# One attention group's values projected ahead of the others, VectorE's exponentials from the first unit on, and the last output tiles spread over three engines

## The chip, the cores and the metric

The kernel runs on one core of a Trainium2 chip. The metric is the device time of one execution in microseconds (us); where a kernel ran several times the median is given.

## The reference

One input x (2048 x 512, bf16) goes through two branches, which a gate mixes for each row:

```python
g = sigmoid((x * gate_w).sum(-1, keepdims=True))
qkv = x @ wqkv                     # 32 heads of 16
p = softmax(q @ k.T * 16 ** -0.5)  # for each head, 2048 x 2048
a = concat_heads(p @ v) @ wo
b = (silu(x @ w_gate) * (x @ w_up)) @ w_down   # 512 -> 1792 -> 512
return g * a + (1 - g) * b
```

The costly part is the exponential of 32 x 2048 x 2048 scores.

## The kernel before

The program is laid out by a planner in Python that runs while the program is built. It keeps estimated clocks of TensorE, ScalarE and VectorE and decides what each engine does next. The scores are cut into 32 *units* (a block of 512 queries with a group of four heads). A unit has 16 *slots* (one tile of 128 keys, four heads: four score tiles of 128 x 512). Group 0 comes first for all four query blocks, so units 0 to 3 are slots 0 to 63. Most score tiles go in pairs to ScalarE (`e_t`). Some go in blocks of four to VectorE, which computes the exponential from integer and half-precision operations (`y_t`). Everything else (projections, gated network, output matmuls) is cut into pieces, and a pacer fits them between score matmuls so that each is done by its deadline.

```python
def v_pieces(tt, act_evac=False):      # values of ALL groups for key tile tt
    ... 4 matmuls of 128x512: lhsT=xT[:, dc, tile tt], rhs=wv[:, dc, :]
    # copied to vaug by ScalarE (act_evac) or by VectorE, later
...
# the start: the key group and its bound (the stabiliser of the softmax)
act(out=q0r, in_=qp0, func=ACT.Copy)
for i in range(2):
    vec.tensor_reduce(out=kpart0[:, i:i + 1], in_=kp0[i], op=ALU.max, apply_absolute_value=True)
    v_now(i)                           # value tile i, copied by ScalarE
    act(out=kaug[...half i...], in_=kp0[i], func=ACT.Identity, bias=ones_h[i], scale=1.0)
    ...
v_now(2); (bound matmul bp0); (two additions on VectorE); v_now(3)
...
for tt in range(4, 16):                # the other value tiles, needed at slot tt
    v_chain[tt] = pace.add(v_pieces(tt), 0, tt + 3)
f0, f1 = 44, SLOTS - 8                 # the network is paced from slot 44
...
def to_vector():                       # may VectorE take the next score tile?
    un, at_ = divmod(nxt, 4 * KT)      # unit, position 0..63 in it
    ...
    if not un or at_ > (50 if un < UNITS - 1 else 4) or y_live[0] >= 3 or sum(v[0] for v in vops) > 6:
        return 0
    return 1
...
last_mm(1, on_l)                       # four last matmuls, tq = 0, 1, 2, 3
for tq in range(TQ):
    store(qb * TQ + tq, a_ps[tq], acc[0][:, tq, :], mt[:, tq, :])   # VectorE addition, store by SyncE
```

Of the kernel before, what the change touches and what calls it, by code (L numbers as in the profile page):

```python
# [78 lines left out]
def kernel(  # L79
# [100 lines left out]

    rb = big.tile([P, NB, QBW], BF16, name="rb")
    wv = rb[:, :, :]

    nc.sync.dma_start(out=wv, in_=A_wqkv[:, 2 * D:3 * D].rearrange("(dc p) c -> p dc c", p=P))
    for c0 in (D, 0):
        nc.sync.dma_start(out=wqk[:, :, c0 + 64:c0 + D],
                          in_=A_wqkv[:, c0 + 64:c0 + D].rearrange("(dc p) c -> p dc c", p=P))
# [39 lines left out]
    for g in range(1, G):  # L227

        nc.vector.memset(kaug[:, g, :].bitcast(F32), 1.0019378662109375)
    vaug = big.tile([P, KT, G * 4 * VC + 16], BF16, name="vaug")  # L230
    nc.gpsimd.memset(vaug[:, :, G * 4 * VC:], 0.0)
    nc.gpsimd.memset(
        vaug[:, :, 0:G * 4 * VC].rearrange("p t (h c) -> p t h c", c=VC)[:, :, :, 0:1], 1.0)

# [5 lines left out]
    for h in range(8):  # L240
        c = 2 * (h % 4) + h // 4
        nc.gpsimd.memset(lo_t[:, c:c + 1], float(DH * h))
    far_t = const.tile([P, 8], F32, name="far_t")

    nc.vector.tensor_scalar(out=lo_t[:], in0=lo_t[:], scalar1=pidx[:, 0:1], scalar2=None, op0=ALU.subtract)
    nc.vector.tensor_scalar(out=far_t[:], in0=lo_t[:], scalar1=-float(DH) + 0.5, scalar2=-1.0,
                            op0=ALU.is_gt, op1=ALU.mult)
    nc.vector.scalar_tensor_tensor(out=bsel[:, :], in0=lo_t[:], scalar=0.5, in1=far_t[:],
                                   op0=ALU.is_lt, op1=ALU.mult)
    nc.gpsimd.memset(wo_l[:], 0.0)  # L250
    sbc_t = const.tile([P, P], BF16, name="sbc_t")
    nc.gpsimd.memset(sbc_t[:], 0.0)
# [125 lines left out]
        vec.tensor_scalar(out=kneg[:, b, :], in0=bsel[:, :], scalar1=kb[:, b:b + 1],  # L378
                          scalar2=None, op0=ALU.mult)

    def v_pieces(tt, act_evac=False):
        st = {}

        def pc(h):
            def f():
                if h == 0:
                    st["p"] = m_tile("vp")
                for dc in (2 * h, 2 * h + 1):
                    mm(st["p"][:, 0:D], lhsT=xT[:, dc, tt * P:(tt + 1) * P], rhs=wv[:, dc, :],
                       start=(dc == 0), stop=(dc == DC - 1))  # L390
                spend("F", 2)
                if h == 1 and act_evac:
                    end()
                elif h == 1:
                    later(0.75, end)
            return f

        def end():
            dst = vaug[:, tt, 0:G * 4 * VC].rearrange("p (h c) -> p h c", c=VC)[:, :, 1:1 + DH]
            sv = st["p"][:, 0:D].rearrange("p (h c) -> p h c", c=DH)  # L400
            if act_evac:
                act(out=dst, in_=sv, func=ACT.Copy)
            else:
                vec.tensor_copy(out=dst, in_=sv)
            m_free(plan.pe if act_evac else plan.dve)
        return [(2, pc(0), True), (2, pc(1), False)]


# [311 lines left out]
    def pv(bs, last):  # L720


        un = bs[0] // (4 * KT)
        extra = un < closed
        if extra:
            o = m_tile("x_ps")
        else:
            if un not in o_of:
                while un and un - 1 not in osbs:
                    pay()  # L730
                plan.pe = max(plan.pe, o_end[0])
                o_of[un] = ps_o.tile([P, QBW], F32, tag="o", name="o_ps")
            o = o_of[un]
        for b in bs:
            n, j = b // 4, HEADS[b % 4]
            first = extra or (un, j) not in begun
            begun.add((un, j))
            c0 = (4 * UNIT[un][1] + j) * VC
            if n < KT and n in v_chain:
                force(v_chain[n])  # L740
            mm(o[32 * j:32 * j + 32, :], lhsT=vaug[:, n % KT, c0:c0 + 32], rhs=e_of.pop(b),
               start=first, stop=extra or last, tile_position=(0, 32 * j), skip_group_check=True)
            e_left.pop(b, None)
        spend("C", 1, max(e_end.pop(b, 0.0) for b in bs))
        if extra:
            def add():
                blocks[un] -= 1
                vec.tensor_tensor(out=(of_of if blocks[un] else osbs)[un][:, :], in0=of_of[un][:, :], in1=o[:, :],
                                  op=ALU.add)
                m_free(plan.dve)  # L750
                if not blocks[un]:
                    finish(un)
            later(0.6, add)
# [116 lines left out]
    q0r = work.tile([P, QBW], BF16, tag="qst", name="q0r")  # L870
    kneg0 = mt[:, 3, P:2 * P]
    kneg1 = mt[:, 3, 2 * P:3 * P]
    def v_now(tt):
        for _, f, _ in v_pieces(tt, act_evac=True):
            f()

    act(out=q0r[:, :], in_=qp0[:, :], func=ACT.Copy)
    for i in range(2):
        vec.tensor_reduce(out=kpart0[:, i:i + 1], in_=kp0[i][:, :], axis=AX.X, op=ALU.max,
                          apply_absolute_value=True)  # L880
        vec.tensor_copy(out=ones_h[i][:], in_=onescol[:])
        v_now(i)
        act(out=kaug[:, 0, i * 2 * QBW:(i + 1) * 2 * QBW], in_=kp0[i][:, :], func=ACT.Identity,
            bias=ones_h[i][:, 0:1], scale=1.0)
        if i == 0:
            vec.tensor_scalar(out=kneg1, in0=bsel0, scalar1=kpart0[:, 0:1], scalar2=None, op0=ALU.mult)
            vec.tensor_scalar(out=aq0[:, :].bitcast(U16), in0=q0r[:, :].bitcast(U16), scalar1=0x7FFF, scalar2=None,
                              op0=ALU.bitwise_and)
    vec.scalar_tensor_tensor(out=kneg0, in0=bsel0, scalar=kpart0[:, 1:2], in1=kneg1,
                             op0=ALU.mult, op1=ALU.min)  # L890
    v_now(2)
    bp0 = ps_d.tile([P, QBW], F32, tag="d", name="bp0")
    mm(bp0[:, :], lhsT=kneg0, rhs=aq0[:, :], start=True, stop=True)
    for v in range(2):
# [1 line left out]
    for v in range(2):  # L896
        vec.scalar_tensor_tensor(out=q0[0][:, v, :], in0=bp0[:, :], scalar=vsel[:, v:v + 1],
                                 in1=q0[0][:, v, :], op0=ALU.mult, op1=ALU.add)
    V0 = 4
    v_now(3)  # L900
    plan.dve = plan.act = plan.pe


    pace = Pacer()
    need = {}
    v_chain = {}
    for tt in range(V0, KT):
        v_chain[tt] = pace.add(v_pieces(tt), 0, tt + 3)
    prev = []
    for qb in range(1, QB):  # L910
        d = qb * KT
# [29 lines left out]
    order_ = [(qb, fc) for qb in range(QB) for fc in range(FC)]  # L941
    prev = []
    fin_prev = []
    f0, f1 = 44, SLOTS - 8
    per = (f1 - f0) / QB
    for qb in range(QB):
        a0 = f0 + per * qb
# [65 lines left out]
    def pv_ready(now):  # L1013

        if late and (now is None or late[0][0] <= now):
            un = late[0][1][0] // (4 * KT)
            if un == closed or un < closed and (now is None or m_ready() is not None and m_ready() <= now):
                return late[0][1]
        if done < SLOTS and done // KT == closed and not (now is not None and done in v_chain
                                                          and not v_chain[done].done()):  # L1020
            bs = [b for b in range(4 * done, 4 * done + 4) if b not in vset]
            if all(b in e_of for b in bs) and (now is None or max(e_end[b] for b in bs) <= now):
                if closed in o_of or now is None or (not closed or closed - 1 in osbs) and o_end[0] <= now:
                    return bs
        return None

    def pvs_ready(now):

        k = n = 0
        for ready, bs in late[:2]:  # L1030
            un = bs[0] // (4 * KT)
            if ready <= now and (un == closed or un < closed and k == 0 and m_ready() is not None and m_ready() <= now):
                k += 1
        for n in (done, done + 1):
            if n < SLOTS and n // KT == closed and not (n in v_chain and not v_chain[n].done()):
                bs = [b for b in range(4 * n, 4 * n + 4) if b not in vset]
                if all(b in e_of for b in bs) and max(e_end[b] for b in bs) <= now and (
                        closed in o_of or (not closed or closed - 1 in osbs) and o_end[0] <= now):
                    k += 1
        return min(k, 2)  # L1040
# [27 lines left out]

    def side(most):

        c = pace.next(plan.slot) if pace.credit > 0 else None
        if c is None:
            return None
        mms, _, takes = c.pieces[c.i]
# [11 lines left out]
    def to_vector():  # L1086

        un, at_ = divmod(nxt, 4 * KT)
        if vcur:
            if nxt % 4 in [b % 4 for b in vcur["b"]]:  # L1090
                return 0
            return 2 if at_ >= 4 * KT - 4 * (NV - vcur["i"]) else 1
        if not un or at_ > (50 if un < UNITS - 1 else 4) or y_live[0] >= 3 or sum(v[0] for v in vops) > 6:
            return 0
        return 1

    while nxt < nb:
# [4 lines left out]
        if pairs[0] - min(e_left.values(), default=pairs[0]) >= EB - 1:  # L1102

            for m in (done, done + 1):
                while m in v_chain and not v_chain[m].out():
                    emit_piece(v_chain[m])
            next_pv()
            continue
        room = s_end[pairs[0] % 2] - plan.pe
# [56 lines left out]
    a_ps += [ps_m.tile([P, QBW], F32, tag="m", name="a_l")[:, :] for _ in range(2)]  # L1166

    def last_mm(w, on):
        for tq in range(TQ):
            mm(a_ps[tq][:, 0:D], lhsT=on[:, tq * P:(tq + 1) * P], rhs=wo_l[:, w, :], start=(w == 0), stop=(w == 1))  # L1170
    last_mm(0, osbs[un - 1])
    dt = ps_d.tile([P, QBW], F32, tag="d", name="dt")
# [12 lines left out]
        cs = slice(tq * P, (tq + 1) * P)  # L1185
        vec.tensor_tensor(out=on_l[:, cs], in0=osb[:, cs], in1=rps[:, cs], op=ALU.mult)
    last_mm(1, on_l)
    for tq in range(TQ):
        store(qb * TQ + tq, a_ps[tq], acc[0][:, tq, :], mt[:, tq, :])


# [28 lines left out]
```

## Time and profile before

| | before |
|---|---|
| median of 3 runs | 876.64 us (876.36 to 877.8) |
| span of the profiled run | 872.4 us |
| exponentials on ScalarE / blocks on VectorE | 882 / 71 |
| first exponential begins | 19.27 us |
| last exponential ends | 863.62 us |
| tail from there to the end | 8.8 us |

Three numbers make up the span: the *start* (up to the first exponential), the *middle* (from there to the end of the last one) and the *tail*. I also use one figure for the middle that I worked out from the trace's records. In every profile of this study the median step from the start of one exponential to the start of ScalarE's next instruction is 904 ns. What all steps have beyond 904 ns, added up, I call the *excess*; it is 20.0 us before. The middle is then 904 ns for each exponential, some 26.8 us for the 57 other ScalarE instructions, and the excess.

### The profile page before, as it was taken

What the parts mean: (1) busy time and instruction counts of PE and PEld (TensorE: products, weight loads), DVE (VectorE), ACT (ScalarE), POOL (GpSimd) and SP (SyncE); (2) the same over time, 40 slices, a digit from 0 to 9 for tenths busy, and PEclk for the clock granted to TensorE, in tenths of its full rate; (3) what the DMA queues carried; (4) which work ended last, traced back from release to release, by engine and by line L of the source; (5) the groups of instructions that cost most, each with busy time, mean ns of one, the idle gap of its engine ahead of it and who ended that gap; (6) DMA issues with size and microseconds to landing.
All of it is one profiled execution on the core that took longest, in us unless ns stands there. A gap on an engine that the chain in (4) does not pass through costs nothing.

```text
span 872.4 us, 14196 instructions
## 1 busy us (share of the span) xinstructions
PE 784.8 (90%) x5078; PEld 207.6 (24%) x5168; DVE 786.9 (90%) x1103; ACT 845.4 (97%) x947; POOL 7.1 (1%) x29
## 2 busy tenths in 40 slices
PE   6999999999999899999989888899898989989985
PEld 2222222222222222222222222222222222222221
DVE  6379999999999999999999999999999998999984
ACT  3999999999999999999999999999999999999995
POOL 3000000000000000000000000000000000000000
PEclk9999999999999999999999999999999999999999
DMA  8401121031101112210011121110011121000000
GB/s 208 111 1 28 29 50 38 21 69 28 31 11 26 40 33 73 52 37 11 4 31 31 34 55 45 42 28 4 4 25 36 36 57 48 21 10 4 5 20 24
DMA packets 87535, 31.98 MB, mean 37 GB/s; under 512 B 75120, under 2 KB 87016, under 8 KB 87464
## 3 DMA queue, kind: packets, MB, share of 16 engines
q1 hardware_dynamic: 86408, 30.94, 14.5%
q8 instruction: 40, 0.66, 0.3%
q10 hardware_dynamic: 1056, 0.13, 0.1%
q14 instruction: 31, 0.25, 0.1%
HBM read 20.83 MB, written 2.34 MB: 27 GB/s over the span
## 4 chain that ended last, share of the span: by engine, by line
ACT 42%; PE 34%; DVE 11%; issue 11%; SPq 1%; DMA 0%; ACTq 0%; DVEq 0%
ACT e_t L161 38%; PE s_t L158 13%; PE o_ps L158 7%; DVE y_t L167 5%; PE d_t L158 4%; PE dps L158 3%; ACT th L161 3%; DVE u_t L167 2%; PE gp L158 2%; PE qp L158 1%; PE up L158 1%; SPq L174 1%; PE kp L158 1%; DVE mt L167 1%; PE a_ps L158 1%
## 5 line engine op out<-in xcount | busy, mean ns | idle before, releaser
L161 ACT ACTIVATE e_t<-s_t 128x1024 bf16<-128x1024 f32 x882 | 821.9, 1079 | 4.8 <-PE s_t L158 3.7
L158 PE MATMUL s_t<-qx,kaug 64*128 64x512 bf16 x1656 | 330.1, 384 | 52.8 <-ACT e_t L161 49.5
L167 DVE TENSOR_SCALAR y_t<-d_t 128x512 uint16<-128x512 f32 x284 | 195.2, 687 | 29.7 <-PE d_t L158 26.2
L158 PEld LDWEIGHTS <-kaug 64*128 64x128 bf16 x2048 | 100.0, 93 | 379.4 <-issue 376.3
L158 PE MATMUL o_ps<-e_t,vaug 128*32 128x512 bf16 x1764 | 172.8, 387 | 1.3 <-ACT e_t L161 0.7
L158 PE MATMUL d_t<-qx,kaug 64*128 64x512 bf16 x264 | 99.6, 377 | 0.6 <-DVE y_t L167 0.3
L167 DVE TENSOR_TENSOR y_t<-y_t,u_t 128x2048 uint16<-128x2048 uint16 x71 | 86.6, 1219 | 0.9
L167 DVE TENSOR_TENSOR u_t<-u_t 128x2048 f16<-128x2048 f16 x71 | 86.5, 1218 | 0.8
L167 DVE TENSOR_TENSOR u_t<-u_t,z_t 128x2048 f16<-128x2048 f16 x71 | 86.4, 1217 | 0.4
L158 PEld LDWEIGHTS <-vaug 128*32 128x32 bf16 x2048 | 45.4, 94 | 133.1 <-issue 129.3
L158 PE MATMUL dps<-wd_t,mt 128*128 128x512 bf16 x200 | 62.4, 384 | 3.0 <-issue 3.0
L158 PE MATMUL gp<-xT,wg 128*128 128x512 bf16 x199 | 62.2, 384 | 2.5 <-issue 2.4
L158 PE MATMUL up<-xT,wu 128*128 128x512 bf16 x207 | 62.2, 383 | 2.0 <-issue 1.9
L167 DVE TENSOR_SCALAR y_t<-y_t 128x2048 uint16<-128x2048 uint16 x71 | 48.9, 688 | 1.2
L167 DVE TENSOR_SCALAR u_t<-z_t 128x2048 f16<-128x2048 uint16 x71 | 48.7, 687 | 0.7
L167 DVE TENSOR_SCALAR z_t<-y_t 128x2048 uint16<-128x2048 uint16 x71 | 48.6, 684 | 0.1
L167 DVE SCALAR_TENSOR_TENSOR gs<-th,gp 128x512 bf16<-128x512 bf16 x56 | 38.2, 681 | 4.2 <-ACT th L161 3.7
L167 DVE SCALAR_TENSOR_TENSOR mt<-gs,up 128x512 bf16<-128x512 bf16 x56 | 38.1, 681 | 2.2
L161 ACT ACTIVATE th<-gp 128x512 bf16<-128x512 f32 x56 | 36.4, 650 | 0.0
L158 PEld LDWEIGHTS <-mt 128*128 128x128 bf16 x263 | 16.2, 99 | 42.8 <-issue 36.5
L158 PE MATMUL s_t<-on,kaug 64*128 64x512 bf16 x108 | 21.7, 383 | 3.6 <-ACT e_t L161 3.1
L158 PEld LDWEIGHTS <-wu 128*128 128x128 bf16 x224 | 13.7, 97 | 32.0 <-issue 27.6
(101 smaller groups left out, 347.1 us busy)
## 6 DMA issues: line engine op xcount, KB each, us to landing
wg<-in_B_w_gate_dram SPq DMA_DIRECT2D x56, 128.0 KB
wu<-in_B_w_up_dram SPq DMA_DIRECT2D x56, 128.0 KB
on<-osb SPq DMA_DIRECT2D x120, 16.0 KB
rb<-rr SPq DMA_DIRECT2D x15, 128.0 KB
wd_t<-in_B_w_down_dram SPq DMA_DIRECT2D x1, 1792.0 KB
qx<-qst SPq DMA_DIRECT2D x112, 16.0 KB
out_dram<-o_t SPq DMA_DIRECT2D x12, 128.0 KB
kaug<-on SPq DMA_DIRECT2D x20, 64.0 KB
```

What stands on the lines that cost most here:

```text
L158: ordered(nc.tensor.matmul(*args, **kw))
L161: ordered(nc.scalar.activation(*args, **kw))
L167: return lambda *a, **kw: ordered(f(*a, **kw))
L174: nc.sync.dma_start_transpose(out=xT[:, dc, :], in_=x[:, dc * P:(dc + 1) * P])
```

## The change

The intent: the first four units need the values of group 0 alone. Project these 64 of 512 columns for all 16 key tiles at the start, while VectorE makes the bound. The other groups' values then have time until slot 64. That leaves room for VectorE to take score tiles in the first unit too. At the end, one of four output tiles goes over ScalarE and GpSimd.

```diff
-    nc.sync.dma_start(out=wv, in_=...all 512 value columns...)
+    nc.scalar.dma_start(out=wv[:, :, 0:64], ...)      # first group, early, other queue
+    nc.sync.dma_start(out=wv[:, :, 64:D], ...)
...                                    # (bsel's three small VectorE operations moved behind the start)
+    def v0(t0):                       # 8 key tiles: 32 matmuls of 64 columns, one copy by ScalarE
+        p = m_tile("vp")
+        for i in range(8):
+            for dc in range(DC):
+                mm(p[:, 64 * i:64 * i + 64], lhsT=xT[:, dc, ...], rhs=wv[:, dc, 0:64], ...)
+        act(out=vaug[:, t0:t0 + 8, 0:4 * VC]..., in_=p..., func=ACT.Copy)
...                                    # v_pieces: columns 64 to 511 only, copied by VectorE
-    for tt in range(V0, KT):
-        v_chain[tt] = pace.add(v_pieces(tt), 0, tt + 3)
+    v_rest = [pace.add(v_pieces(tt), 2, int(12 + 3 * tt)) for tt in range(KT)]
...
-    f0, f1 = 44, SLOTS - 8
+    f0, f1 = 72, SLOTS - 8
...
+        due = any(not c.out() for n in range(plan.slot, plan.slot + 12) for c in need.get(n, []))
-        c = pace.next(plan.slot) if pace.credit > 0 else None
+        c = pace.next(plan.slot) if pace.credit > 0 or due else None
...
-        if not un or at_ > (50 if un < UNITS - 1 else 4) or ...
+        if nxt < 16 or at_ > (50 if un < UNITS - 1 else 12) or ...
...
-        for tq in range(TQ):                                  # last matmuls
+        for tq in (2, 0, 1, 3):
...
+    act(out=scaled, in_=a_ps[2], func=ACT.Identity, scale=gval[:, t:t + 1])
+    nc.gpsimd.tensor_tensor(out=mt[:, 2, :], in0=scaled, in1=acc[0][:, 2, :], op=ALU.add)
-    for tq in range(TQ):
+    for tq in (0, 1, 3):
         store(...)
+    nc.sync.dma_start(out=out_f[t * P:(t + 1) * P, :], in_=mt[:, 2, :])
```

The `due` line lets the pacer's next piece go although its credit is used up, when something that is needed within 12 slots isn't out yet.

More of the change, by code (lines that the diff above doesn't have):

```diff
@@ L182 @@
     wv = rb[:, :, :]
-    nc.sync.dma_start(out=wv, in_=A_wqkv[:, 2 * D:3 * D].rearrange("(dc p) c -> p dc c", p=P))
+    nc.scalar.dma_start(out=wv[:, :, 0:64], in_=A_wqkv[:, 2 * D:2 * D + 64].rearrange("(dc p) c -> p dc c", p=P))
+    nc.sync.dma_start(out=wv[:, :, 64:D], in_=A_wqkv[:, 2 * D + 64:3 * D].rearrange("(dc p) c -> p dc c", p=P))
     for c0 in (D, 0):
@@ L231 @@
     nc.gpsimd.memset(vaug[:, :, G * 4 * VC:], 0.0)
+    nc.gpsimd.memset(vaug[:, :, 4 * VC:4 * VC + 16], 0.0)
     nc.gpsimd.memset(
@@ L243 @@
     far_t = const.tile([P, 8], F32, name="far_t")
-    nc.vector.tensor_scalar(out=lo_t[:], in0=lo_t[:], scalar1=pidx[:, 0:1], scalar2=None, op0=ALU.subtract)
-    nc.vector.tensor_scalar(out=far_t[:], in0=lo_t[:], scalar1=-float(DH) + 0.5, scalar2=-1.0,
-                            op0=ALU.is_gt, op1=ALU.mult)
-    nc.vector.scalar_tensor_tensor(out=bsel[:, :], in0=lo_t[:], scalar=0.5, in1=far_t[:],
-                                   op0=ALU.is_lt, op1=ALU.mult)
     nc.gpsimd.memset(wo_l[:], 0.0)
@@ L379, in k_bound, with v_pieces @@
                           scalar2=None, op0=ALU.mult)
-    def v_pieces(tt, act_evac=False):
+    def v0(t0):
+        p = m_tile("vp")
+        for i in range(8):
+            for dc in range(DC):
+                mm(p[:, 64 * i:64 * i + 64], lhsT=xT[:, dc, (t0 + i) * P:(t0 + i + 1) * P], rhs=wv[:, dc, 0:64],
+                   start=(dc == 0), stop=(dc == DC - 1))
+        act(out=vaug[:, t0:t0 + 8, 0:4 * VC].rearrange("p t (h c) -> p t h c", c=VC)[:, :, :, 1:1 + DH],
+            in_=p[:, :].rearrange("p (t h c) -> p t h c", h=4, c=DH), func=ACT.Copy)
+        m_free(0.0)
+    def v_pieces(tt):
         st = {}
@@ L388, in f @@
                 for dc in (2 * h, 2 * h + 1):
-                    mm(st["p"][:, 0:D], lhsT=xT[:, dc, tt * P:(tt + 1) * P], rhs=wv[:, dc, :],
+                    mm(st["p"][:, 64:D], lhsT=xT[:, dc, tt * P:(tt + 1) * P], rhs=wv[:, dc, 64:D],
                        start=(dc == 0), stop=(dc == DC - 1))
                 spend("F", 2)
-                if h == 1 and act_evac:
-                    end()
-                elif h == 1:
-                    later(0.75, end)
+                if h == 1:
+                    later(0.7, end)
             return f
         def end():
-            dst = vaug[:, tt, 0:G * 4 * VC].rearrange("p (h c) -> p h c", c=VC)[:, :, 1:1 + DH]
-            sv = st["p"][:, 0:D].rearrange("p (h c) -> p h c", c=DH)
-            if act_evac:
-                act(out=dst, in_=sv, func=ACT.Copy)
-            else:
-                vec.tensor_copy(out=dst, in_=sv)
-            m_free(plan.pe if act_evac else plan.dve)
+            dst = vaug[:, tt, 4 * VC:G * 4 * VC].rearrange("p (h c) -> p h c", c=VC)[:, :, 1:1 + DH]
+            vec.tensor_copy(out=dst, in_=st["p"][:, 64:D].rearrange("p (h c) -> p h c", c=DH))
+            m_free(plan.dve)
         return [(2, pc(0), True), (2, pc(1), False)]
@@ L738, in pv @@
             c0 = (4 * UNIT[un][1] + j) * VC
-            if n < KT and n in v_chain:
-                force(v_chain[n])
+            if v_of(n) is not None:
+                force(v_of(n))
             mm(o[32 * j:32 * j + 32, :], lhsT=vaug[:, n % KT, c0:c0 + 32], rhs=e_of.pop(b),
@@ L872 @@
     kneg1 = mt[:, 3, 2 * P:3 * P]
-    def v_now(tt):
-        for _, f, _ in v_pieces(tt, act_evac=True):
-            f()
     act(out=q0r[:, :], in_=qp0[:, :], func=ACT.Copy)
@@ L881 @@
         vec.tensor_copy(out=ones_h[i][:], in_=onescol[:])
-        v_now(i)
         act(out=kaug[:, 0, i * 2 * QBW:(i + 1) * 2 * QBW], in_=kp0[i][:, :], func=ACT.Identity,
@@ L885 @@
         if i == 0:
-            vec.tensor_scalar(out=kneg1, in0=bsel0, scalar1=kpart0[:, 0:1], scalar2=None, op0=ALU.mult)
             vec.tensor_scalar(out=aq0[:, :].bitcast(U16), in0=q0r[:, :].bitcast(U16), scalar1=0x7FFF, scalar2=None,
                               op0=ALU.bitwise_and)
+        v0(8 * i)
+    vec.tensor_scalar(out=kneg1, in0=bsel0, scalar1=kpart0[:, 0:1], scalar2=None, op0=ALU.mult)
     vec.scalar_tensor_tensor(out=kneg0, in0=bsel0, scalar=kpart0[:, 1:2], in1=kneg1,
                              op0=ALU.mult, op1=ALU.min)
-    v_now(2)
     bp0 = ps_d.tile([P, QBW], F32, tag="d", name="bp0")
@@ L898 @@
                                  in1=q0[0][:, v, :], op0=ALU.mult, op1=ALU.add)
-    V0 = 4
-    v_now(3)
+    vec.tensor_scalar(out=lo_t[:], in0=lo_t[:], scalar1=pidx[:, 0:1], scalar2=None, op0=ALU.subtract)
+    vec.tensor_scalar(out=far_t[:], in0=lo_t[:], scalar1=-float(DH) + 0.5, scalar2=-1.0,
+                            op0=ALU.is_gt, op1=ALU.mult)
+    vec.scalar_tensor_tensor(out=bsel[:, :], in0=lo_t[:], scalar=0.5, in1=far_t[:],
+                                   op0=ALU.is_lt, op1=ALU.mult)
     plan.dve = plan.act = plan.pe
@@ L905, with v_of, v_done @@
     need = {}
-    v_chain = {}
-    for tt in range(V0, KT):
-        v_chain[tt] = pace.add(v_pieces(tt), 0, tt + 3)
+    v_rest = [pace.add(v_pieces(tt), 2, int(12 + 3 * tt)) for tt in range(KT)]
+    def v_of(n):
+        return v_rest[n - QB * KT] if QB * KT <= n < QB * KT + KT else None
+    def v_done(n):
+        return v_of(n) is None or v_of(n).done()
     prev = []
@@ L1018, in pv_ready @@
                 return late[0][1]
-        if done < SLOTS and done // KT == closed and not (now is not None and done in v_chain
-                                                          and not v_chain[done].done()):
+        if done < SLOTS and done // KT == closed and (now is None or v_done(done)):
             bs = [b for b in range(4 * done, 4 * done + 4) if b not in vset]
@@ L1034, in pvs_ready @@
         for n in (done, done + 1):
-            if n < SLOTS and n // KT == closed and not (n in v_chain and not v_chain[n].done()):
+            if n < SLOTS and n // KT == closed and v_done(n):
                 bs = [b for b in range(4 * n, 4 * n + 4) if b not in vset]
@@ L1092, in to_vector @@
             return 2 if at_ >= 4 * KT - 4 * (NV - vcur["i"]) else 1
-        if not un or at_ > (50 if un < UNITS - 1 else 4) or y_live[0] >= 3 or sum(v[0] for v in vops) > 6:
+        if nxt < 16 or at_ > (50 if un < UNITS - 1 else 12) or y_live[0] >= 3 or sum(v[0] for v in vops) > 6:
             return 0
@@ L1104 @@
             for m in (done, done + 1):
-                while m in v_chain and not v_chain[m].out():
-                    emit_piece(v_chain[m])
+                while v_of(m) is not None and not v_of(m).out():
+                    emit_piece(v_of(m))
             next_pv()
@@ L1187 @@
     last_mm(1, on_l)
-    for tq in range(TQ):
+    t = qb * TQ + 2
+    scaled = work.tile([P, QBW], F32, tag="of", name="scaled", bufs=1)
+    act(out=scaled[:, :], in_=a_ps[2][:, 0:D], func=ACT.Identity, scale=gval[:, t:t + 1])
+    nc.gpsimd.tensor_tensor(out=mt[:, 2, :], in0=scaled[:, :], in1=acc[0][:, 2, :], op=ALU.add)
+    for tq in (0, 1, 3):
         store(qb * TQ + tq, a_ps[tq], acc[0][:, tq, :], mt[:, tq, :])
+    nc.sync.dma_start(out=out_f[t * P:(t + 1) * P, :], in_=mt[:, 2, :])
 _INS = ['A_x', 'A_wqkv', 'A_wo', 'B_x', 'B_w_gate', 'B_w_up', 'B_w_down', 'gate_w']
```

## The prediction

> **What bounds the kernel now.** I read the page first: shares of busy time, the 40 slices and the costliest groups.
>
> ```profile
> PE 784.8 (90%) x5078; PEld 207.6 (24%) x5168; DVE 786.9 (90%) x1103; ACT 845.4 (97%) x947; POOL 7.1 (1%) x29
> DVE  6379999999999999999999999999999998999984
> ACT  3999999999999999999999999999999999999995
> L161 ACT ACTIVATE e_t<-s_t 128x1024 bf16<-128x1024 f32 x882 | 821.9, 1079 | 4.8 <-PE s_t L158 3.7
> L167 DVE TENSOR_SCALAR y_t<-d_t 128x512 uint16<-128x512 f32 x284 | 195.2, 687 | 29.7 <-PE d_t L158 26.2
> ```
>
> ScalarE is full in every slice but the first and the last, and 882 exponentials of two 128x512 score tiles each are nearly all it does; in the whole span they waited 4.8 us. The other 284 score tiles (4 x 512 heads and key tiles make 2048 = 2 x 882 + 284) have their exponential computed on VectorE, in 71 blocks of four. VectorE is full too, except in the slices with 6, 3 and 7 at the start. So time has three terms: when the first exponential starts, how many exponentials ScalarE must do, and the tail after the last.
>
> Second, the stretches of time (columns: stretch, its length, busy us and instructions of PE, PEld, DVE, ACT, POOL, clock, DMA share, GB/s):
>
> ```profile
> 20.00:30.00 10.00, 9.00 (x56) 2.56 (x58) 2.77 (x4) 10.00 (x12) 0.00 (x0) 1.00 0.99 265
> 30.00:40.00 10.00, 9.44 (x58) 2.46 (x62) 5.32 (x8) 10.00 (x12) 0.00 (x0) 1.00 0.00 1
> 40.00:60.00 20.00, 18.94 (x120) 4.77 (x119) 11.62 (x19) 19.38 (x22) 0.00 (x0) 1.00 0.01 1
> 60.00:80.00 20.00, 19.52 (x132) 4.96 (x129) 19.69 (x29) 20.00 (x23) 0.00 (x0) 1.00 0.11 22
> ```
>
> VectorE works 19.7 of the 40 us from 20 to 60 while ScalarE is full: about 20 us of VectorE in which no score tile is taken off ScalarE. The tile view says the same: the first score tile goes to VectorE at 47.9 us, when the second unit begins, because the kernel forbids it in the first.
>
> Third, the chain at the start and the time line of the two ends:
>
> ```profile
> 10.20 4.05 DMA rb<-in_A_wqkv_dram
> 14.29 1.04 PE vp L158 x4
> 15.35 0.60 ACT vaug L161
> 15.95 1.00 ACT kaug L161
> 17.44 1.01 ACT kaug L161
> 18.45 0.97 ACT vaug L161 x2
> ...
> 16.88 0.38 PE L158 MATMUL bp<-aq,mt 128*128 128x512 bf16 x1
> 17.30 1.41 DVE L167 SCALAR_TENSOR_TENSOR qx<-bp,vsel,qx 128x512 bf16<-128x512 f32 x2 [0.50 <-PE bp L158]
> ...
> 866.92 1.41 DVE L167 SCALAR_TENSOR_TENSOR mt<-al,gval,kaug 128x512 bf16<-128x512 f32 x2
> 867.70 2.31 SPq L823 DMA_DIRECT2D out_dram<-mt  x4
> 868.24 1.40 DVE L167 SCALAR_TENSOR_TENSOR mt<-a_l,gval,kaug 128x512 bf16<-128x512 f32 x2
> ```
>
> The load of the value weights (rb) lands at 14.25 us. ScalarE runs in order, so the first value tile, which waits for it, holds back the keys' copy, and the first exponential starts at 19.27. A second chain is almost as late: bound matmul at 16.88, VectorE's two additions to 18.71, scores. At the end the last exponential is over at 863.6; four output additions and four stores follow.
>
> **What the Trainium skill says.** "ScalarE: Activation LUTs", section "What ACT_TABLE_LOAD costs", gives 186 ns + 0.833 ns an element with immediate operands, about 93 ns more for a [128,1] pointer, and an overlap of about 93 ns back to back. For 1024 elements that is 1039 and 946 net. The trace has 1079 in the mean and steps of 0.91 to 0.92 us between exponentials: the step agrees within 4% and is what counts here. "TensorE: Matmul & The Clock Gate", section "Back-to-back issue gap", says that a matmul of 1 to 64 columns costs about 25 ns at least, and that a stream of load and matmul pairs at 128 columns takes about 81 ns. The gate's matmuls (128x1, a fresh 128x128 load each) agree with the lower one: eight in 0.35 us, starts about 30 ns apart. "GPSIMD Engine Reference", section "Elementwise — side-by-side cycle accounting", gives 2.6 cycles of 1.2 GHz an element for a two-input add, and that the engine can't read PSUM. This trace has no such add. "DMA: Bandwidth & Descriptors", section "Anatomy of one DMA", gives some 2 us of fixed cost; the first 64 KB weight piece, issued on ScalarE's queue at 0.80, was used at 3.13, which agrees.
>
> **The change part by part.**
>
> (a) Start. The first group's 64 value columns come as a third 64 KB load on ScalarE's queue, issued at about 1.8 and landed by 6 or 7 (the second, issued at 1.25, was used at 5.05), so the wait to 14.25 goes. It moves bytes forward into the transposed loads: two such pieces are 2.8% of 16 engines over 30 us, 0.84 us, so one costs at most 0.4 us; I charge 0.2. Four value projections of 16 wide matmuls (16 x 0.216 = 3.5 us of TensorE) become two of 32 narrow ones: at 30 to 55 ns each 1.0 to 1.8 us, so from 13.56 (end of the query matmul) the first is done at 14.6 to 15.3 and the second at 15.5 to 17.1. ScalarE: query copy to 14.2, keys' first half from 14.35 (its VectorE operand is there at 14.3) to 15.4, value copy 0.5, second half 1.0, value copy 0.6: free at 17.5 to 17.7, not 19.4. VectorE: reduce ends at 14.2; the three small bsel operations leave the path (0.3 us), the scaling of 0.24 joins its end, so the negated bound is ready at about 16.3, as before. The bound matmul then starts at 16.4 if the narrow matmuls are through, at 17.1 if not (before: 16.88). The scores need its first addition: bound + 0.4 + 0.7 + 0.4 + 0.3, so the first exponential at 18.2 to 18.9. Gain 0.4 to 1.1, less 0.2: I take 0.6.
>
> (b) The first unit on VectorE. Permission from the fifth slot (about 26 us) and values of the other groups spread to slot 57 instead of 15, and the gated network's pacing moved from slot 44 to 72. A block costs VectorE 4 x 0.61 + 3 x 0.60 + 3 x 1.23 = 7.9 us in steps and in 28 of 71 blocks an extra add: 8.2. It saves ScalarE two exponentials, 1.83. To be had are the 20 us of idle time at the 95% that VectorE reaches from 120 us on, 19.0, less new work: 16 value copies of 448 columns (about 0.61, scaled from 0.69) for 12 of 512, +1.5 us: 17.5. But an end that comes 1.83 us sooner per block takes 0.95 x 1.83 = 1.7 us of VectorE away. So n = 17.5 / (8.2 + 1.7) = 1.8 blocks: 2 as a whole number, ScalarE -3.6 us. That is all on the path, as ScalarE waits for nothing. Shifting the network changes no sum of work; its matmuls come 115/108 as densely (6%), on a TensorE with 6 to 10% idle from 200 us on.
>
> (c) Other ScalarE work before the first exponential is counted in (a). The last unit may begin a block up to position 12, not 4; the old kernel did begin one there (y_t written from 833.8 to 841.1), so nothing is added.
>
> (d) Tail. VectorE's additions go from four to three: -0.7. But the matmuls' new order 2, 0, 1, 3 needs the third product first, some 0.2 later, and the first addition reads the second matmul: another 0.2. Tile 2 goes over ScalarE (0.65 to 0.7) and then GpSimd: my estimate from the GPSIMD page is 512 x 2.6 / 1.2 = 1.1 us plus some 0.2, so done at about 867.15 + 0.7 + 0.1 + 1.3 = 869.3. Its store is issued last, behind tile 3's near 869.4, half a microsecond per issue: 869.9, where the old last issue ended at 870.0. Gain 0.1, so 0.
>
> Sum: -0.6 - 3.6 - 0.0 = -4.2 us on 876.64: 872.4.
>
> **The rivals.** First: TensorE becomes the bound in the opening. For it: it is 90 to 95% busy there, and from 40 to 73 us the chain hops over its matmuls. Against it: the value tiles (12 x 4 x 0.216 = 10.4 us) are thinned out over three times as many slots, and ScalarE's waits there are 0.4 us. If true, the blocks cost stalls and the gain is 1 to 2 us: 875. Second: VectorE's time is only moved, so that values, keys and the denser network take back later what the first unit gave: n = 1 or 0, 874 to 876. For it: VectorE is at 95% later; against it: the idle 20 us are really idle. Third: the opening takes three or more blocks as later units leave fewer holes (VectorE lost 26 us waiting for d_t): n = 3 or 4, 868.5 to 870.5. Fourth: narrow matmuls at 81 ns or more, 64 x 0.081 = 5.2 us, push the bound matmul to 18.8 and the first exponential past 20.5: start +1.3 and total 874.3. Fifth: the last head of the first group reads 16 columns which the other groups' copies now write later, so value matmuls and those copies wait for each other; each wait is short and off ScalarE's path unless its twelve buffers fill up. Sixth: GpSimd's add is much slower than estimated and its store sets the end: +1 us per extra us.
>
> **Range and chances.** n = 1, 2, 3 give 874.2, 872.4, 870.5 with the start as taken; start and tail add about 1 us either way, and the runs before spread over 1.4 us. I say 872.4, with 869.0 to 875.4 eight times in ten. A change of 2% is 17.5 us, over nine blocks: faster by 2% 0.02, within 2% 0.97, slower 0.01.
>
> **What would show it.** Right: 878 exponentials and 73 blocks (292 d_t tiles, the first at 26 to 30 us), VectorE at 8 or more tenths from 30 to 60 us, ScalarE's idle still near 5 us, the first exponential at 18.2 to 18.9, narrow vp matmuls 30 to 55 ns apart, 8.5 to 9 us from the last exponential to the end. Wrong: 880 or more exponentials (n too large), ScalarE waiting for s_t between 20 and 120 us (first rival), a first exponential after 19.3 (a), or a last store that waits for GpSimd (d).

## The result

Before 876.5 us and after 872.15 us, medians of six runs each; the ratio is 0.9954 (95% interval 0.9937 to 0.9972). A ratio here is the mean time of one kernel's fast runs over that of the other's in the same rounds, so it isn't quite the ratio of the medians. The predicted 872.4 is met within 0.3 us. The three parts of the two profiled runs show that the sum was not reached in the way that the prediction gave.

| profiled run | start | exponentials | middle | excess | tail | span |
|---|---|---|---|---|---|---|
| before | 19.27 | 882 | 844.4 | 20.0 | 8.8 | 872.4 |
| after | 18.26 | 880 | 841.8 | 19.3 | 9.7 | 869.8 |
| predicted difference | -0.6 | -4 | -3.6 | 0 | 0 | -4.2 |
| measured difference | -1.0 | -2 | -2.5 | -0.7 | +0.9 | -2.6 |

The two profiled spans differ by 2.6 us, the medians by 4.35. The profile of before is of an execution of 874.11 us, faster than all six timed ones. Differences of this size come with variations that the profiles below show: when the first loads land, how soon TensorE's first matmuls run at full speed, and dips of the granted clock.

First the page of the changed kernel: VectorE's 40 slices, and the two groups that did the exponentials.

```profile
DVE  7889999999999999999999999989999999998974
L161 ACT ACTIVATE e_t<-s_t 128x1024 bf16<-128x1024 f32 x880 | 819.6, 1090 | 5.4 <-PE s_t L158 4.8
L167 DVE TENSOR_SCALAR y_t<-d_t 128x512 uint16<-128x512 f32 x288 | 197.8, 687 | 28.3 <-PE d_t L158 24.5
```

The slices that held 3 and 7 are at 8 and 9 now, but there are only 72 blocks (288 tiles), one more than before. The stretches say where VectorE's time went, before and then after (columns as in the prediction: length, busy us of PE, PEld, DVE, ACT, POOL).

```profile
20.00:60.00 40.00, 37.38 (x228) 9.79 (x231) 19.70 (x31) 39.38 (x44) 0.00 (x0) 1.00 0.25 67
60.00:120.00 60.00, 56.00 (x386) 15.30 (x386) 57.34 (x82) 60.00 (x68) 0.00 (x0) 1.00 0.12 26
120.00:850.00 730.00, 666.18 (x4328) 173.75 (x4403) 685.52 (x937) 725.83 (x815) 0.00 (x0) 1.00 0.13 31
```

```profile
20.00:60.00 40.00, 38.45 (x246) 10.56 (x245) 35.52 (x52) 39.78 (x45) 0.00 (x0) 1.00 0.25 67
60.00:120.00 60.00, 58.00 (x403) 16.47 (x402) 55.86 (x81) 59.99 (x67) 0.00 (x0) 1.00 0.07 14
120.00:850.00 730.00, 681.33 (x4412) 173.50 (x4411) 683.81 (x933) 725.43 (x817) 0.00 (x0) 1.00 0.13 32
```

From 20 to 60 us VectorE gained 15.8 us of work; from 60 to 850 us it lost 3.2 us. The count of blocks by unit agrees: 2 blocks in the first unit instead of 0, and 70 in the other 31 units instead of 71.

The start after, as a chain and as a time line:

```profile
7.90 4.66 DMA xT<-in_A_x_dram
12.60 0.60 PE kp L158 x2
13.23 1.22 DVE kpart L167
14.80 1.13 DVE kpart L167
17.03 1.41 DVE qx L167 x2
```

```profile
13.68 2.03 PE L158 MATMUL vp<-rb,xT 128*128 128x64 bf16 x64
```

The value weights and ScalarE's copies have left the chain. It now runs from the last slice of x over the key matmuls, two reductions and two additions on VectorE. The 64 narrow value matmuls take 2.03 us, 32 ns each, and lie beside the reductions.

The tail after (start, duration, engine, what):

```profile
863.13 0.39 PE L158 MATMUL a_l<-wo_l,on_l 128*128 128x512 bf16 x1 [0.79 <-DVE on_l L167]
863.56 0.69 ACT L161 ACTIVATE scaled<-a_l,gval 128x512 f32<-128x512 f32 x1 [3.47 <-PE a_l L158]
863.99 1.41 DVE L167 SCALAR_TENSOR_TENSOR mt<-al,gval,kaug 128x512 bf16<-128x512 f32 x2 [0.72 <-PE al L158]
864.33 1.26 POOL L1199 TENSOR_TENSOR mt<-scaled,kaug 128x512 bf16<-128x512 f32 x1 [856.03 <-ACT scaled L161]
865.32 0.74 DVE L167 SCALAR_TENSOR_TENSOR mt<-a_l,gval,kaug 128x512 bf16<-128x512 f32 x1
865.62 0.36 SPq L1202 DMA_DIRECT2D out_dram<-mt  x1
866.08 1.37 SPq L826 DMA_DIRECT2D out_dram<-mt  x3
```

The store of tile 2 (L1202) is last in the source, but it is issued first, at 865.62, when GpSimd's add is done. The other three follow it, though tile 0 had been ready since about 864.7. So the slowest tile's store appears to have held back the others; e2 tests that. Why the built program has it first is not shown.

### The profile page after: what moved, and what is told of

Read it like the earlier page. It is cut to its first block, busy times and chain, and to the rows that moved or that the text cites. A ratio compares the mean times of both kernels' runs of the same rounds, so it can differ in the third digit from the quotient of the medians.

```text
span 869.8 us, 14419 instructions
## 1 busy us (share of the span) xinstructions
PE 798.7 (92%) x5232; PEld 208.8 (24%) x5232; DVE 796.5 (92%) x1117; ACT 842.7 (97%) x944; POOL 8.6 (1%) x31
## 4 chain that ended last, share of the span: by engine, by line
PE 46%; ACT 35%; DVE 8%; issue 8%; SPq 1%; DMA 1%; DVEq 0%; ACTq 0%
ACT e_t L161 33%; PE s_t L158 17%; PE o_ps L158 9%; PE dps L158 5%; PE d_t L158 4%; DVE y_t L167 4%; PE gp L158 3%; ACT th L161 3%; PE up L158 2%; DVE u_t L167 2%; PE a_ps L158 1%; PE qp L158 1%; PE vp L158 1%; PE kp L158 1%; PE x_ps L158 1%
## 5 line engine op out<-in xcount | busy, mean ns | idle before, releaser
L158 PE MATMUL s_t<-qx,kaug 64*128 64x512 bf16 x1648 | 326.7, 384 | 47.7 <-ACT e_t L161 44.6
L167 DVE TENSOR_SCALAR y_t<-d_t 128x512 uint16<-128x512 f32 x288 | 197.8, 687 | 28.3 <-PE d_t L158 24.5
L158 PE MATMUL d_t<-qx,kaug 64*128 64x512 bf16 x272 | 102.5, 377 | 0.6 <-DVE y_t L167 0.6
L158 PE MATMUL dps<-wd_t,mt 128*128 128x512 bf16 x224 | 67.8, 384 | 0.0
L158 PE MATMUL gp<-xT,wg 128*128 128x512 bf16 x224 | 67.8, 384 | 0.0
L158 PE MATMUL up<-xT,wu 128*128 128x512 bf16 x224 | 64.7, 383 | 0.0
```

What stands on the lines that cost most here:

```text
L158: ordered(nc.tensor.matmul(*args, **kw))
L167: return lambda *a, **kw: ordered(f(*a, **kw))
```

## The experiments

Each kernel had six runs, in rounds with the kernel before, and one profile. The runs came in four calls on three chips (e0 to e3; e4, e5, e7 and e9; e6, e10 and e8; e11), so between calls the ratio to before is the safer measure. The parts, in the order in which they are told (the first row repeats the changed kernel):

| kernel | median | ratio to before | start | exps | middle | excess | tail |
|---|---|---|---|---|---|---|---|
| e0 changed kernel again | 872.29 | 0.9961 | 18.92 | 880 | 842.2 | 19.7 | 9.7 |
| e1 old tail | 871.0 | 0.9951 | 18.76 | 880 | 840.7 | 18.1 | 8.7 |
| e2 store on ScalarE's queue | 871.25 | 0.9947 | 18.36 | 880 | 840.7 | 18.1 | 8.7 |
| e3 no first unit on VectorE | 873.72 | 0.9976 | 19.31 | 882 | 842.2 | 17.7 | 10.9 |
| e4 before + first unit | 875.02 | 0.9994 | 20.96 | 878 | 841.6 | 21.0 | 10.5 |
| e5 values alone | 885.94 | 1.0113 | 18.95 | 882 | 856.7 | 32.2 | 8.7 |
| e7 more blocks | 876.69 | 1.0016 | 18.93 | 876 | 845.4 | 26.6 | 10.7 |
| e9 load later | 872.56 | 0.9969 | 18.77 | 880 | 842.8 | 20.4 | 9.7 |
| e6 old pace | 879.86 | 1.0052 | 19.00 | 880 | 849.6 | 27.1 | 9.7 |
| e10 values soon | 873.13 | 0.9975 | 18.48 | 880 | 842.2 | 19.7 | 9.7 |
| e8 best | 867.31 | 0.9908 | 18.64 | 878 | 836.7 | 16.0 | 10.0 |
| e11 best, tile 2 | 868.15 | 0.9915 | 20.52 | 878 | 836.7 | 16.0 | 9.75 |

**e0: the changed kernel again.** No edit.

> The changed kernel again, as the yardstick of this call. My theory: three terms against the kernel before, each read from the profile: first exponential 1.0 us sooner (18.3 against 19.3), two exponentials fewer (880 against 882, one more block on VectorE: -1.8), and a tail from the last exponential's end to the end that is 0.9 us LONGER (9.7 against 8.8): about -2 to -4 us in all, ratio 0.995 to 0.998. A rival that puts the gain down to a tail shortened by the three engines expects a tail below 8.8 us.

The three terms came again: 880 exponentials, tail 9.7, and a start at 18.92. In both profiles of this kernel the first exponential begins 5.66 us after the last key matmuls, which wait for the last slice of x (12.60 there, 13.26 here). Before it was 6.95 us after 12.32. So the chain was shortened by 1.3 us, and when the last slice of x is there shifts the whole. The excess also repeats to 0.1 us in most stretches of 50 us, with one exception in each. In the changed kernel's first profile 1.3 us more fell between 800 and 850 us, where the granted clock was 0.91 in the last 20 us of that stretch. In this one 1.5 us more fell before 50 us, where the clock was 0.95. Without such a dip the excess of this program is 18.1 us, as e1 and e2 have it.

**e1: the old tail.**

```diff
-        for tq in (2, 0, 1, 3):
+        for tq in range(TQ):
...
-    (tile 2 over ScalarE and GpSimd, three additions, store of tile 2)
+    for tq in range(TQ):
+        store(qb * TQ + tq, a_ps[tq], acc[0][:, tq, :], mt[:, tq, :])
```

> The changed kernel with the old ending: four additions on VectorE in the order 0, 1, 2, 3, four stores in that order. Theory: the split lost time, since the store of tile 2 stands first in SyncE's queue and holds the other three until GpSimd is done; so the tail goes back to 8.7 to 8.9 us and the kernel is 0.9 us FASTER than the changed one. Rival (the split gains 0.7 us of VectorE as intended): 0.1 to 0.7 us slower than the changed one. Middle as in the changed kernel: 880 exponentials.

The tail is 8.70 us, a full microsecond shorter, and the median 1.3 us lower. The split over three engines, as made, lost time.

**e2: the store of tile 2 on another queue.**

```diff
-    nc.sync.dma_start(out=out_f[t * P:(t + 1) * P, :], in_=mt[:, 2, :])
+    nc.scalar.dma_start(out=out_f[t * P:(t + 1) * P, :], in_=mt[:, 2, :])
```

> The changed kernel with only the store of tile 2 issued from ScalarE's queue instead of SyncE's. Theory (queue order is what costs): the stores of tiles 0, 1, 3 are issued as each addition ends, the last near 6.1 us after the last exponential instead of 7.0, and the tail is 8.7 to 8.9 us, 0.8 to 1.0 less than the changed kernel's 9.7. Rival (GpSimd's add or the reordered matmuls cost the time): the tail stays above 9.4 us.

The time line of its end:

```profile
863.27 1.26 POOL L1199 TENSOR_TENSOR mt<-scaled,kaug 128x512 bf16<-128x512 f32 x1 [854.95 <-ACT scaled L161]
863.71 1.65 SPq L826 DMA_DIRECT2D out_dram<-mt  x3
864.57 0.37 ACTq L1202 DMA_DIRECT2D out_dram<-mt  x1
```

SyncE's three stores now begin before GpSimd is done (864.53), and the tail is 8.71 us. That is the 1.0 us: the order in the queue cost it. With that gone the split merely equals the old tail, as the prediction had it. The first addition begins about 0.6 us later by the new order of matmuls, which eats the addition saved.

**e3: the first unit forbidden to VectorE again.**

```diff
-        if nxt < 16 or at_ > (50 if un < UNITS - 1 else 12) or ...
+        if not un or at_ > (50 if un < UNITS - 1 else 12) or ...
```

> The changed kernel with VectorE's exponentials forbidden in the first unit again; all else as changed. It plans 71 blocks, 882 exponentials. Theory (the count of exponentials is on the path): 1.8 us slower than the changed kernel, with the first exponential and the tail as there. Rival (the gain comes from thinning the value matmuls out of the opening, not from the block): within 0.5 us of the changed kernel. If it is 3 us slower or more, more than the count is at work, such as ScalarE's waits for scores later on.

By the medians it is 1.4 us slower than e0 (the intervals of the ratios overlap), which looks like the 1.8 us expected. The parts say otherwise. The middle is 842.16 us against 842.18 in e0, with a clock of 0.95 from 18 to 50 us in both, although two exponentials more were done: the excess is 2.0 us smaller. The loss is in the tail, 10.9 against 9.7, where the last unit's block came so late that its sum was still to be added after the last exponential. So the count of exponentials is not the time: two exponentials less were paid for in waits. Nor did the middle need the first unit's blocks: with the same 882 exponentials as before it is 2.2 us shorter than before's 844.4.

**e4: the kernel before, with the first unit permitted.**

```diff
-        if not un or at_ > (50 if un < UNITS - 1 else 4) or ...
+        if nxt < 16 or at_ > (50 if un < UNITS - 1 else 4) or ...
```

> The kernel before, with VectorE's exponentials permitted in the first unit from the fifth slot; value projection, pacing and ending as before. It plans 73 blocks, 878 exponentials. Count theory (904 ns of ScalarE for each exponential, all on the path): the stretch from the first exponential to the end of the last shrinks by 4 x 0.904 = 3.6 us, the kernel is 3.6 us faster than before. Rival (the first unit's VectorE and TensorE have no room while twelve value tiles are still to be projected there, so exponentials wait for scores): the sum of ScalarE's steps over 904 ns grows from about 19 us by 2 us or more and the gain is under 1.5 us. Start 19.3 and tail 8.8 as before in both.

Two blocks more, four exponentials fewer, and the medians are 875.02 and 875.46: nothing that can be told from zero. The middle is 2.7 us shorter and not 3.6, as the excess grew by 1.0 (by 2.2 if some 1.2 us are left out that fell between 800 and 850 us in the profile of before, whose clock too was 0.91 from 830 to 850). That 2.2 is what the rival said, and as much arose from 40 to 80 us, where the excess is 3.9 here, 1.6 before and 0.6 in the changed kernel's first profile. The start and the tail were longer in the profiled run. The granted clock was 0.69 from 850 us on, which is not of the edit's making as far as I can show. The start is of interest, because it is the old one, at its worst; its chain:

```profile
10.44 5.51 DMA rb<-in_A_wqkv_dram
15.99 1.04 PE vp L158 x4
17.05 0.60 ACT vaug L161
```

The value weights landed at 15.95 us here, against 14.25 in the profile of before, and the first exponential began 1.7 us later, at 20.96. So the old start hung on a load whose landing differed by 1.7 us between two profiles, and removing that wait can be worth more than the one profile of before showed.

**e5: the value projection alone.** The first unit forbidden, the network paced from slot 44, the old ending and its old limit of 4; the values as changed, and the `due` line kept.

```diff
-        if nxt < 16 or at_ > (50 if un < UNITS - 1 else 12) or ...
+        if not un or at_ > (50 if un < UNITS - 1 else 4) or ...
-    f0, f1 = 72, SLOTS - 8
+    f0, f1 = 44, SLOTS - 8
     (old tail as in e1)
```

> The changed kernel with only the value projection kept (first group at once, others thinned out): no exponentials on VectorE in the first unit, the network paced from slot 44, the old ending. It plans 71 blocks, 882 exponentials, as before. Count theory: only the start gains: the first exponential at 5.7 us after the last slice of x is used instead of 7.0, so 0.5 to 1.3 us faster than before. Rival (taking value matmuls out of the opening is itself worth waits for scores): ScalarE's steps over 904 ns add up to 1.5 us or more less than before's, and the kernel is 2.5 us or more faster than before although the count is the same.

Both theories missed: it is about 10 us slower than before, with the same count. The waits from 20 to 850 us:

```profile
ACT e_t L161 <- PE s_t L158: 14.1, 16, 4.5
PEld L158 <- DVE kneg L167: 7.6, 2, 4.0
PE bp L158 <- DVE kneg L167: 6.8, 2, 3.5
```

`kneg` is the key bound of a later group, made on VectorE, and `bp` the matmul that uses it. TensorE stood 3.3 us before the `bp` at 147.8 us and 3.6 us before the one at 205.2. The score matmuls came only after these, and ScalarE ran dry: its exponentials at 148.8 and 206.4 had waited 3.1 and 4.5 us. No `bp` waited for `kneg` in the profiles of before and after.

**e7: more blocks.**

```diff
-        if nxt < 16 or at_ > (50 if un < UNITS - 1 else 12) or ...
+        if nxt < 16 or at_ > (54 if un < UNITS - 1 else 12) or ...
```

> The changed kernel with blocks allowed to begin until position 54 of 64 in a unit, not 50. It plans 74 blocks, 876 exponentials. Count theory: 4 x 0.904 = 3.6 us faster than the changed kernel. Rival (VectorE is full, so a block more is bought with waits of ScalarE): ScalarE's steps over 904 ns add up to 3 us or more above the changed kernel's 18, and the kernel is no faster than it, or slower.

Two blocks more than changed, 3.6 us of ScalarE less by count, and the kernel is 4.4 us slower than e0 (1.0 of it in the tail, where the last block ended late as in e3). The waits of the changed kernel and then of this one, from 20 to 870 us:

```profile
ACT e_t L161 <- PE s_t L158: 4.2, 10, 0.7
PE d_t L158 <- DVE y_t L167: 0.6, 1, 0.6
```

```profile
ACT e_t L161 <- PE s_t L158: 10.0, 14, 1.8
PE d_t L158 <- DVE y_t L167: 7.7, 12, 1.0
```

TensorE now stands 7.7 us for VectorE to empty the one score buffer that it reads (`d_t`), and passes the wait on to ScalarE. So with this limit more blocks cost more than they bring. That VectorE has no room left at all doesn't follow: e8 fits one more in.

**e9: the small load behind the slices of x.**

```diff
-    nc.scalar.dma_start(out=wv[:, :, 0:64], ...)
+    nc.sync.dma_start(out=wv[:, :, 0:64], ...)   # same line, now behind the transposed loads
```

> The changed kernel with the first group's value weights (64 KB) loaded behind the four transposed loads on SyncE's queue, no longer ahead on ScalarE's. Theory (the early small load delays the transposed slices of x, whose last was used at 12.6 to 13.7 us in five profiles against 12.3 before): the last key matmuls begin at 12.2 to 12.5 and the first exponential, 5.7 us later, at 17.9 to 18.2. Rival (the slices land late by chance of the runs, not because of the load): they begin at 12.6 to 13.7 again. If the load itself lands after 13.7 us, the narrow matmuls wait for it and the gain is lost.

A miss: the last key matmuls began at 13.11 us, as late as with the early load, and the time is that of the changed kernel. The early small load is not shown to delay the slices. In twelve of the fourteen profiles the last key matmuls waited for the last slice, until 12.32 to 13.34 us. In e3 and e11 they waited for no slice: they began at 13.48 and 14.02 us, behind key matmuls that ran 0.41 to 0.43 us apart, where the others' last ones ran 0.215 apart.

**e6: the network paced from slot 44.**

```diff
-    f0, f1 = 72, SLOTS - 8
+    f0, f1 = 44, SLOTS - 8
```

> The changed kernel with the gated network paced from slot 44 again, not 72; 72 blocks and 880 exponentials as there. My prediction's step (moving the network changes no sum of work): within 0.7 us of the changed kernel, ScalarE's steps over 904 ns again 18 to 19 us without a clock dip. New theory from the run with the value projection alone, where 12 us were lost as TensorE stood waiting for the key bound: an early network crowds keys, bounds and thinned values between 90 and 250 us, so ScalarE's steps over 904 ns grow by 3 us or more there and the kernel is 3 us or more slower than the changed one.

7.6 us slower than e0, with the same count, start and tail. The excess is 27.1 us; between 150 and 250 us it is 8.1 where the changed kernel has 1.6. Another 2.6 us fall after 850 us (0.2 in e0), where the granted clock was 0.66 from 850 to 860. The waits from 150 to 250 us:

```profile
PEld L158 <- DVE kneg L167: 3.6, 2, 1.9
ACT e_t L161 <- PE s_t L158: 2.9, 2, 2.5
PE bp L158 <- DVE aq L167: 2.2, 1, 2.2
```

Again TensorE stands at the bound matmul for VectorE. As I read the planner, an early network, with the other groups' values thinned out to slot 57, pushes keys, queries and their bounds past the slot at which they are forced; no run shows that link by itself. So the one-line shift to slot 72 is not a neutral retiming: without it the other parts lose more than they win.

**e10: the other groups' values soon.**

```diff
-    v_rest = [pace.add(v_pieces(tt), 2, int(12 + 3 * tt)) for tt in range(KT)]
+    v_rest = [pace.add(v_pieces(tt), 2, int(4 + tt)) for tt in range(KT)]
```

> The changed kernel with the other groups' values no longer thinned out: due from slot 4 to 19 (as before), not 12 to 57. It plans 72 blocks, 880 exponentials. If thinning is what makes room for the first unit's blocks: ScalarE waits for scores in the first 60 us, its steps over 904 ns exceed 0.7 us there by 1.5 us or more, and the kernel is 1.5 us or more slower than the changed one. If it is the first group's early projection that matters (no exponential's use waits for a value tile any more) and not the thinning: within 0.7 us of the changed kernel.

0.8 and 1.0 us slower than the changed kernel's two medians, just outside the 0.7 said, with overlapping intervals of the ratios. The parts look like e0's, but e0's excess holds 1.5 us of a clock dip. Against the 18.1 without a dip the excess is 1.6 higher here, nearly all of it after 100 us (the clock was 0.97 from 100 to 150). Before 50 us it is 1.0, not 2.2 or more. So it is not the thinning that makes the room in the opening. That no early exponential waits for a whole value tile any more is left as the likely reason, and not tested by itself.

**e8: a version to beat both.**

```diff
-    v_rest = [pace.add(v_pieces(tt), 2, int(12 + 3 * tt)) for tt in range(KT)]
+    v_rest = [pace.add(v_pieces(tt), 2, int(12 + 2 * tt)) for tt in range(KT)]
     (last matmuls in the order 0 to 3; tile 0, not 2, over ScalarE and GpSimd)
+    nc.scalar.dma_start(out=out_f[t * P:(t + 1) * P, :], in_=mt[:, 0, :])
```

> A version meant to beat both: the changed kernel with matmuls and additions of the last tiles in the order 0 to 3, tile 0 over ScalarE and GpSimd, its store on ScalarE's queue; and the other groups' values due at 12 + 2 per tile instead of 12 + 3. It plans 73 blocks, 878 exponentials. Tail: 8.3 to 8.6 us (first addition 0.4 us sooner than in the changed kernel, three additions, no store held back), 1.1 to 1.4 less than the changed kernel. Middle: by count 1.8 us less; by the waits theory between 1.8 less and 1 more. In all 1 to 3 us faster than the changed kernel, 868 to 871 us.

867.31 us, ratio 0.9908: 8.5 us below before and 5 below e0, where 1 to 3 were expected. From its page:

```profile
L161 ACT ACTIVATE e_t<-s_t 128x1024 bf16<-128x1024 f32 x878 | 817.0, 1084 | 2.6 <-PE s_t L158 1.5
L167 DVE TENSOR_SCALAR y_t<-d_t 128x512 uint16<-128x512 f32 x292 | 200.3, 686 | 27.4 <-PE d_t L158 24.1
```

Here a block more did come without waits: ScalarE waited 1.5 us for scores, not 4.8, and the excess is 16.0. The middle is 5.1 us shorter than in the first profile of the changed kernel, and 4.0 shorter than in e1 and e2, where the clock didn't dip. Why this deadline hits it and another does not is not explained; I chose it because the planner gave 73 blocks with an early end of its plan. The tail was expected at 8.3 to 8.6 and is 10.0. The last unit's block ended late, as in e3. The last four matmuls' first addition also stood 0.8 us for ScalarE, which scaled the tile beside it.

**e11: the same with tile 2.**

```diff
-    (tile 0 over ScalarE and GpSimd, tiles 1, 2, 3 on VectorE)
+    (tile 2 over ScalarE and GpSimd, tiles 0, 1, 3 on VectorE)
```

> The best version so far with tile 2 instead of tile 0 over ScalarE and GpSimd (matmuls stay in the order 0 to 3, its store stays on ScalarE's queue). In the version so far VectorE's first addition waited 0.8 us for ScalarE's scaling of tile 0, which lies in the same tile of PSUM. If that wait is the cost: the first addition begins 0.4 us after the first of the last four matmuls, not 1.1, and the tail from the end of the last exponential shrinks from 9.95 to 9.2 to 9.6 us; the time falls by 0.3 to 0.7 us, to 866.6 to 867.0. If another step sets the end (GpSimd's 1.26 us now come later), the tail stays within 0.2 us. The middle is the same: 878 exponentials, ScalarE's steps over 904 ns 15 to 16 us.

The wait is gone, and the first addition begins 0.4 us after the first matmul, but the tail is only 0.2 us shorter (9.75). Tile 2 is made later, so GpSimd ends at 863.98, and its store now goes last with tile 3's. The median is 868.15, not below e8's, and the two ratios can't be told apart. The profiled start was 20.52, behind the slow key matmuls told under e9; how many of the timed runs had that isn't known. The middle repeats to 0.02 us, which shows how fixed the schedule is once it is built.

## Why the prediction was right, and where it was not

The number and the range were right. Of its four steps (a) was right in kind and too small, (c) held as far as the planner shows, (b) and (d) failed, and what was missed on one side made up for the other. That the sum agreed is luck. Two of the signs of being wrong that it had named came: 880 exponentials, and stores that waited for GpSimd.

- **(a) Start, predicted -0.6.** Right in mechanism. The wait for the value weights left the chain; bound and scores came as computed, and the narrow matmuls at 32 ns each are at the low end of the 30 to 55 given. From the last slice of x the chain is 1.3 us shorter (6.95 to 5.66). The profiled start was 1.0 us sooner, at 18.26 in the range given; with the last slice used at 12.32, as before, it would have been 17.98, below the range. The 0.2 us charged for the small load isn't shown (e9). What was missed is that the load which the old start waited for varies: it landed at 14.25 us in one profile and 15.95 in another, with starts at 19.27 and 20.96.
- **(b) "That is all on the path, as ScalarE waits for nothing."** This step failed. The first unit gave its two blocks as said, but the sum over units was 1. Of the 19.0 us of VectorE counted on, 15.8 came and 3.2 were given back after 60 us; less the 1.5 of new work that leaves 11.1, which is one block of 8.2 and not two. (VectorE's share from 120 to 850 us was 93.9%, not the 95% used.) And a block isn't worth 1.83 us by itself. With the permission withdrawn the middle was the same (e3). Two blocks more than before brought the old kernel nothing (e4), and two more than changed cost it 4.4 us (e7). The term that the sum left out is the excess, 16 to 32 us by schedule; its moves were as large as the count's.
- **(b) "Shifting the network changes no sum of work."** True of the work and wrong for the time. Undone alone, it costs 7.6 us (e6): TensorE then stands at bounds that VectorE hasn't made yet. That the deadlines are why is read from the planner.
- **(c) Last unit, predicted 0.** With the limit of 4 put back into the changed kernel the planner builds the very same program, so there was nothing to run.
- **(d) Tail, predicted 0.** Failed: +0.9. The parts were sized well (GpSimd 1.26 us against 1.3, first addition 0.6 later against 0.4). The step "its store is issued last" was wrong; it was issued first and held the others (e1, e2).
- **The rivals.** The first (TensorE as the bound of the opening) didn't come about. The second (VectorE's time only moved) is partly what happened: n = 1, and 3.2 us given back after 60 us. The third didn't come about. The fourth was refuted by the 32 ns and the sixth by the 1.26 us. For the fifth, the profile of after shows no instruction that waited for one of the other groups' value copies from 18 to 130 us.

Middle and start made the gain, against the tail. What share of the middle's 2.5 us belongs to which line of the diff can't be given: the parts act through one schedule and don't add up. By e3 it doesn't hang on the first unit's permission.

## What to carry to other kernels

In a schedule that a planner makes in advance, a freed engine is worth what the *next* forced wait allows: read the waits of the engine that feeds the bound (here TensorE standing for a VectorE result), not the idle share of the engine to be filled. When work at the end is spread over engines, put the slowest piece's store on a queue of its own: here one store waiting at the head of the queue held back those behind it, which cost 1.0 us. And before calling a prediction right, split the time into parts and compare each: here the sum agreed within 0.3 us while two of four steps were wrong.

## What the Trainium skill lacked or had wrong

- "TensorE: Matmul & The Clock Gate", section "Back-to-back issue gap": it gives about 25 ns as the floor to 64 columns and 81 ns sustained for load and matmul pairs of 128 columns, but nothing sustained for pairs of 64. Here 64 such pairs, each with a fresh 128x128 load, took 2.03 us, 32 ns each.
- "DMA: Bandwidth & Descriptors", section "Anatomy of one DMA — SWDGE (gpsimd) path": it says that a wait is held on the issuing sequencer, which is what cost 1.0 us here, but doesn't warn that stores which are ready stand behind one that isn't (tile 0's, ready at about 864.7, followed tile 2's, issued at 865.62). Moved to another queue, the tail went from 9.7 to 8.7 us.
- None of the pages that I read says how much the landing of the first loads varies between runs of one program: the matmuls that waited for the last slice of x began at 12.32 to 13.34 us in twelve profiles, the value weights landed at 14.25 and at 15.95 us with the same start code, and the first exponential moved with them.
